# An attention block and a gated MLP on one core: the verdict's bound taken from sums on the squarings, w_out loaded through GpSimd's queue, a new instruction order, and the general path as loops

## The chip, the cores and the metric

The kernel runs on one core of a Trainium2 chip. A core has five engines with queues of their own: TensorE (PE in the profile; its weight loads are PEld), VectorE (DVE), ScalarE (ACT), GpSimd (POOL) and SyncE (SP), which here only issues DMAs. The metric is the device time of one execution, in microseconds; it is the median of three runs.

## What is computed

```python
def _attn_ref(x, inducing):            # x: 4 x 12416 x 128, inducing: 32 x 128
    def mab(q, kv):
        s = scale * (q @ kv.transpose(0, 2, 1))
        s = s - s.max(-1, keepdims=True)
        a = np.exp(s)
        a /= a.sum(-1, keepdims=True) + 1e-09
        return a @ kv
    h = mab(I, x)                      # 32 rows h for each of the 4 batches
    return mab(x, h)                   # each token of x attends to the 32 rows of h

def _moe_ref(x, w_gate, w_val, w_out): # 128 -> 1536 -> 128, on all 49664 tokens
    gate = np.maximum(x @ w_gate, 0.0)
    val = x @ w_val
    return gate * val @ w_out
```

All inputs and the output are float32.

## The kernel before

**The method.** A token's attention output is a convex combination of the 32 rows of h, with weights p. The MLP of it has a product of two linear terms, and a relu. The kernel assumes that each of the 1536 gate units has one sign for all rows of h of a batch; then relu drops out and the output is a quadratic form in p. It is written with squares of differences p_i - p_k, of which there are 16 x 32 for a token, times a table T that depends on the batch alone. So the work is done in two parts. For each batch: the sums over all tokens that give h ("centre"), gates and values of the 32 rows (`gates`, `values`), products of them (`product`, tiles U), `joined` (adds the two halves of U, or leaves the sum to TensorE), `table` (matmuls with wo into T), and a linear part (`lin`, tiles lt, then L). For each block Q of 2048 tokens (24 of them, and one block for the four remainders): the scores s2, `s2_exp` (p on ScalarE), p squared (pp), the normaliser z and its reciprocal (zr), the differences by a matmul with a constant matrix (`differences`, for j = 0 to 3, four PSUM banks each), their squares F, and `outputs` (17 matmuls for each quarter of the block), which `divide` scales into osb, and a store.

**Who squares.** Of the four banks of a (Q, j), the tile dd holds two, which ScalarE squares in one instruction (`sq_two`). Each of the other two (`sq_one`) is squared by ScalarE, or cast by VectorE to SBUF and multiplied there by GpSimd or VectorE (`sq_mul`).

**The verdict.** The assumption on signs is verified while the kernel runs: `extreme` takes the largest absolute score of each block (rng, VectorE); `ext1` to `ext3` make a bound on the scores into a condition on the gates; `other` looks at sums and reciprocals; `count` and `verdict` write one number, left. At the end every engine loads left and branches: if it isn't zero, `general_kernel` computes everything again without the assumption. With these inputs the branch skips it.

**The order.** Within the main stage the order on each engine isn't left to a scheduler. `Plan.add` registers each step with the engines that may run it, the steps that must come before, and the buffer slots that it uses. `ORDER`, a long string of base-64 digits that was made outside the kernel, lists the steps in order, with the engine and the slot of each, and fillers (matmuls that only keep TensorE's clock up, `keep_busy`). Each engine works through its own list in order.

**The start.** `first_batch` handles batch 0: x comes in parts on SP's queue as float32, GpSimd and ScalarE cast it, TensorE turns it and makes the sums. Behind x on SP's queue come w_gate, w_val and w_out as float32 (three tiles w32), which are cast to wg, wv and wo:

```python
        nc.gpsimd.tensor_copy(out=wg, in_=w32[0])
        load_x(1, 0, x16q[0])
        nc.gpsimd.tensor_copy(out=wv[:, 0:half], in_=w32[1][:, 0:half])
        nc.scalar.copy(out=wv[:, half:], in_=w32[1][:, half:])
        for q in range(1, NQ + 1):
            load_x(1, q, x16q[q] if q < NQ else x16r[1])
            if q == 2:
                nc.gpsimd.tensor_copy(out=wo, in_=w32[2].rearrange("p (i c) -> p i c", c=P))
```

`load_x` reads x of the next batch through GpSimd's queue, with a cast to float16 on the way; SP turns it by DMA transposes. The tiles of the main stage (pool mp: ga, va, U, p, F, gm and others) take the memory of `first_batch`'s pool sp (x0, w32, p1a) once it is released.

Lines of the profile that are spoken of: 415, 417, 418, 422 the casts of the weights; 207 `load_x`; 771 `gates`; 785 the gate means gm; 490 `s2_exp`; 503 `extreme`; 541 `differences`; 550 `sq_two`; 555 and 557 `sq_one` on ScalarE and VectorE; 561 `sq_mul`; 569 and 581 `outputs`; 591 `divide`; 361 and 905 ScalarE's exponentials of the first batch and its share of the tables; 874 `product`; 888 `joined`; 893 `table`; 1008 in `other`; 1026 `verdict`; 1278 the branch.

Of the kernel before, what the change touches and what calls it, by code (L numbers as in the profile page):

```python
# [81 lines left out]
0W00X0KV4A1j201t004531K021v11x21V011u10Y01y31W00q4Ka4B0Z21X01Y01n004521Z223O0011L01o11M03P2KH0110f4
3Q2KC0001p11N0KI12V0421O21KD1KJ012X11a021r11b02W21c01d0KR0101e2KE05KS11P041f4KF2KM002KK22Y322300051
KN1KT012522411Q0KW0122631R0KX11S0KO001T2271KY02KP22E051U4KU22F0KZ22u0040A29012v12w2Kn32A0Kb002Ko312
y22B02x3Kc12G02i0040B2H02m1Kd022z32I232k12C02P00Ke22j12D22Z052Ku302K042a22L0K+332J4Kj22M02o00219Kk2
2N02b32p1L432Kl052O202Q0LA342R0Km22s12S02c00347LG352q149010LM32g12d12e2NC02NF042T22f3NE1N805NH14+03
2N922U4NG1NB2N400501NA23E04N52N72ND1330551304-24B1340N623503604A23R00234NJ32+0037223V12-03S1300310N
S239013T14D0303F03G0NR23H03d005253A03I21NL33e13B03C0322NK33D23X004003843f24C323Z1520123J43Y15323b23
g34E23h23jA05463c25p0113l1NT23k13n23i35r14S90038NW24T1LN45q23o34U14W24GA0253NM33p044H14K2Kp42NV2NN0
14I1NU2Kv413q0NQ243003r04M00351NO24X3K-404404N13s04Q23u024L33t233v04O13+05L544NP13-0Ne24Y004324004Z  # L90
1410NI2Kq011LB4342205s313w0Kr13x04504c24a1Nf054F3Ks01542NY2Ng0LH455H0034BNj1Kt24d34603y25L1NZ01Na05
I14723z44R37T050Kw004Nd24845J15B00209NX2Kx14e015D14p035F2Nq37V14f04g04h05C17U2L00144q04i224r0L114s0
5N002074t21L2055P14j015R25O14k0Nk2Nr04Ns0550032A5G2Nv1Ky005S35915725t0414l05614m0Kz24u025u25834n26e
0325w00046L324o46g1Nl017W325+25y1Nm0L60155x16f2LV3LI0045v34v05-2L714w0LW314x0Np160000344y2LJ1L805Lc
336415e01622Li304z46i0406115Y02L926336j25j035f05g0Nw266000555k06k36716A25l0Lo325m05h05n23LC0146B368
15T055i2LD15U06h306C003005o4LE046D16G28I011Lu345V0LF25W08K16H26x000426E15Z05X205a06y15b06-26T036U05
c27036z16V06r005438J25d47X0226N006s16t26O06P07Y26Q06v16u26l001586R227Z36Y026m16p26I046Z06n18L316W07
1000516X216J0731970126q37526K07216L06a06M26b0763LO0139917m000576c2LP1LK046S47n1982LQ036d47C02L+35LL
27D07o17q2M439W0014B7I00LR29X17r39a29B05177039C27809Y1LS27a004599D37909b37b17c27A0LT017B237J07e17K0
7d27L07g0043ALU27E07k17F07N057i17O09A307P07h17M207Q0O603N-047R2O71O301O81Nx00O22O417S4O027s00530Ny2  # L100
O517G27u19y0107w27H48M0207t1Nz27x3O12M549+18N28PA0535N+2OB27y048Q1OJ27z0LX467+07-08R1OI28V002048T18
1058W180228O3OC3820Ld478309z284087038X1OA38528808Z18b00416890Lj498c18f28A08C02OD38B218D08d18E08h005
019-22Lp488F08g38i18l2An011OE038G28j19E004088m2Lv4AAp1LY002OF29F18s05Ao28t08u0OO28v0OG1L-4B9G1Ar012
8y03LZ18z08w20Le0149I18n02O928H4Lf1864OK28o09K0050291049L1OL28p08q09209O1As2Aq319308r2940La0195238x
4A3000238+0At2A71A52Lk0048-0A41Lb2Lg02A639M2Ll1Lq0109029N39Q00150Lh2Lr1Lm049649U29R1Bc032Ls02Ln29V2
Lw0009S1Lt2A900547OM2Lx1A00209n01AD19s00A12OH2Be19o0Ly02AA1Bd2A239p09t09u0Lz2Au0043AOP2M0012Aw19v0O
N29q0Ay1OQ04M11OR09r21Oh3OV0OW03Av1OX09w2OY0OZ0OU29x4AB2AF002199h00Oa2AG1AJ29i09j09k0AH1M6004BA0053
1Ob2M71Oi01BE1Oj09l22BB1Oc02Od0Om2AK2M8049c03Og2BC2AL000159d0On2AN19e09f0AM1CR020Bf20M2059g2BD3AP1M
32Bg0019m4B400354M92CT1Bh2MA2B51AC2MB01CS2Bi3Ah04B81MC2Ai0B61A+00026Aj0B01AR05A-1AS0B22Oo03AT0AU0Op
2B33Or2Ew001Oq2Bj0012BAV20Ey1Oz03Ak0Bn1Bl2BR05O+1BS0Al23Bk1Bm3BT0BU0Ex2Os02Ow01O-1Ov2BG04Ox1Ot2BV21  # L110
Bp00032Oy1BH0P02Br1BI0BJ0Ou2Bq1BL01BK22BM0BN0PD2Bt1BO0B-00508AW02C31P12AX0C01BP2AY0AZ0Ac04PA2BQ4C11
Ad0Bv00300Ae0CU22Bx1DG012Bz2Af0Bw1BW05P82BX0BY0DI1CY00303Ag2Ez31BZ0CZ1DH2Am4B+3Cc2Ca1DTA0415Aa2Cd3C
A00DU1Ba2Ab4CG03PE2DX1Bb4CB0CC0Cq00257DV1DK010P92CD0Cu1CL04Cr1CM0CE22CV052CN0CO0DL2CH0Cs1CW2P22CI0C
k00019PB2CJ0Cl1C505CK23CX3PM0C60DJ30C70Cm1C80CP2Ce00231PG0Co2PH00CQ4Ci1PI0PC2Cf1PJ0PK0E5040P32PL1DN
00134PF2Cg1PN00DO1PO0DR2Cp3PP0PQ0E71DP2Df00236P43PY0PR2DA01Dg1E62DB0PS3C92P500Dj1Dh1CF4EO0045AP62Cw
03EP1Cx0ES2DC0DD0P71Cy0EQ1DE20EC00258Cz0ET3ED1PT00C+21PU0C-04EG1PX2DZ0013BDS2EE1D500DQ2Da1Db2D60E83
2D70D80Ga052Dd1D92EU00212Dc3Gc1D00D10DF4EV1D20Gb2Ge031PZ00Gf2Pa0EY1DM2D32Gn00530EW1Pb0Gp2D44Dq01Go1
Gr2Pc0Dw04Pd2Gt00257Gq2Dx0Gs2Gu1Dy0Gv2Dz0Dl03D+23Gx1Gw3Dm0FJ00029Dn0FK1FN2Do0E9042D-05EA2FO3Dp22E00
FL1F700241E10F81F92E20Gd30Dr0Ds0E32Dt0FB1EI00303FA3Du2E44Fl020EJ1EM2Dv4E+050E-2Fn1EN2FD90416EB2Pe2E
K1FE1FF2F03El90Pi2Eq05FH1Fy0034BEr0FG3Fz1F+2Es0Et0Em0Fm2En0G01Eo0F-3Eu20G200135Ef02G31Ep2Eg0Eh0Gg2E  # L120
i0Ev4G61Ea04Ej21G41F100504Fo32Eb0F21F32Ec0HP031Ed0F42HR1G800218Ee2F51GC2G91Fp052Ek4FU04Fq2GD2FV0FW0
GA1HQ2Fr3Ho00012FX0Hp1Hq2Ff05Fg0FY23Fh0Hs1Fi0HW0023AHr2Fa00Fj22HX1Fb0Fc0Fd0Ha1FP04Fe2HY1Fs00153FQ0H
S21Fk4Ft1Ju030Fw2FR0FS0Fu1Fx2Gh00024FT2Jw1GJ05Gi1Jv2FZ4GK0Gj2GL0GM0Gl1Hi00149Gk3GN20HT030GU00Hj1HU2
GV0Hm2GW0GX0Hk1HV2Gz00256Hn3GY21GP03G+1H12GQ0GR0GS0G-2J3042H23Hc00101GT2J51GE05Hd1H03He2GF0GZ4GG0GH
0J42IE021Hg1Hf3JS00313GI2IG1HJ04JW2JT1GO4HK0J632HL0IF2HM0Hu00JU1HN22JX3JA00518H802Pf2JB1H90JE2HA0HB
0JC1Hv0HC23Hw0JF3JM00345Hx0JN1JO2HE01HF0Hy21HG0JQ1HH0IX0052BJP2I303HI2IZ1I40Ib1I50HO4I60H300IY1I720
H40H50Jx20H60J7042Hz01H72JG00524J82H+0HD4JI1J93H-0I00JH1I803I12I90IA0IH21JK1IB0I24IL00046IC2Jy051Jo
01IM1IN2Jp0ID4Jq0Jd02Jz2IP1IO2Id00300J+3Jj05Ie1If2Je0Jf0Ih2Jg0JY04Jh22IR00307JZ0Ig2IS1Ja0Ii2Jb0II02
0Jr0Jc2Jk0IT1Jl0Jm0IJ2IV1Ji4Js23Pg04IK3J-00322Ph2Ij00K31Io01K01Jn2Ik0Ip0Iq0Pj2Jt4Ir0K12Il0Im0Is21Iu
02Iv0In2Iw0Ix0Iz04K22It4Iy20I+0I-0J00K505J12K60K70K80J24Pk03K922Pl2KA4Pm4"""  # L130


# [5 lines left out]
def square_body(ctx, tc, x, inducing, moe_w_gate, moe_w_val, moe_w_out, out):  # L138
# [100 lines left out]
    def first_batch(sp, psum):  # L239
# [179 lines left out]
        for q in range(1, NQ + 1):  # L419
            load_x(1, q, x16q[q] if q < NQ else x16r[1])  # L420
            if q == 2:
                nc.gpsimd.tensor_copy(out=wo, in_=w32[2].rearrange("p (i c) -> p i c", c=P))  # L422
# [887 lines left out]
```

## Time and profile before

| | |
|---|---|
| median of three runs | 269.79 us (269.72 to 269.85) |
| the profiled execution | 270.34 us, its span 268.6 us |
| granted TensorE clock, mean | 0.945 |
| busy: PE, DVE, ACT, POOL | 239.6, 229.3, 198.7, 124.3 us |
| first divide (line 591) | at 52.47 us |
| last divide ends | at 261.1 us |
| read from and written to HBM | 27.80 and 25.43 MB |

The span is the time between the first and the last instruction of the profiled execution. A row of a group reads: line, engine, operation, output <- inputs, shapes, count, then busy us, mean ns of one, and the idle time of the engine just before with what ended it.

### The profile page before, as it was taken

The numbers are of one execution on the slowest core, as the hardware profiler recorded it, in microseconds if no ns is written. First come the engines' busy times: TensorE is split into PE (matmuls) and PEld (weight loads), VectorE is DVE, ScalarE is ACT, GpSimd is POOL, SyncE is SP. The second block draws the span as 40 slices with busy tenths as digits, with TensorE's granted clock in tenths as the row PEclk, the third lists the DMA queues.
The fourth block names the chain that finished last, engine by engine and source line by source line (L and its number), as shares of the span: only waits on it lengthen the run. The fifth ranks groups of instructions, "written<-read, shape, count | busy, mean of one in ns | idle before, by whom it ended". The sixth has DMA issues, their size and how long they took to land.

```text
span 268.6 us, 9038 instructions
## 1 busy us (share of the span) xinstructions
PE 239.6 (89%) x3825; PEld 170.3 (63%) x3825; DVE 229.3 (85%) x468; ACT 198.7 (74%) x321; POOL 124.3 (46%) x146
## 2 busy tenths in 40 slices
PE   6797588999996889999989999999999989999980
PEld 2685235577662467777756878675767656667770
DVE  4655899976799998978999999999988998997980
ACT  3564677775877358878898798899989889987710
POOL 4456604334875947765655244224483631380000
PEclk9999559999998589999999999999999999999995
DMA  7999994995899589999989992104423224333462
GB/s 254 414 397 272 207 214 93 263 246 153 182 265 243 172 190 194 329 201 276 301 257 214 198 368 93 78 2 195 198 81 124 87 109 159 159 156 159 187 270 68
DMA packets 52624, 53.90 MB, mean 201 GB/s; under 512 B 39744, under 2 KB 41952, under 8 KB 52576
## 3 DMA queue, kind: packets, MB, share of 16 engines
q1 hardware_dynamic: 49504, 43.69, 52.0%
q0 software_dynamic: 3024, 9.54, 19.2%
q8 instruction: 32, 0.52, 0.8%
q14 instruction: 16, 0.13, 0.2%
q10 hardware_dynamic: 48, 0.02, 0.0%
HBM read 27.80 MB, written 25.43 MB: 198 GB/s over the span
## 4 chain that ended last, share of the span: by engine, by line
PE 53%; DVE 28%; DMA 8%; ACT 4%; issue 2%; SPq 1%; POOL 1%; DVEq 0%; ACTq 0%; POOLq 0%
PE mb L581 25%; DVE U L874 8%; PE mb L569 8%; PE dd L541 7%; DMA x<-in_x_dram 6%; DVE osb L591 5%; DVE F L557 4%; PE mb L671 2%; DVE U L888 2%; ACT F L550 2%; PE mb L893 2%; PE mb L686 2%; PE mb L481 2%; DMA xT<-x16q 2%; DVE rng L503 1%
## 5 line engine op out<-in xcount | busy, mean ns | idle before, releaser
L550 ACT ACTIVATE F<-dd 128x1024 f16<-128x1024 f32 x97 | 99.7, 1028 | 22.6 <-PE mb L541 19.8
L581 PE MATMUL mb<-T,F 128*128 128x128 f16 x1552 | 113.8, 221 | 0.0
L581 PEld LDWEIGHTS <-F 128*128 128x128 f16 x1552 | 96.3, 99 | 22.9 <-issue 11.3
L561 POOL TENSOR_TENSOR F<-F 128x512 f16<-128x512 f16 x50 | 56.0, 1127 | 52.8 <-DVE F L557 49.0
L555 ACT ACTIVATE F<-mb 128x512 f16<-128x512 f32 x118 | 68.7, 602 | 11.8 <-PE mb L541 11.6
L591 DVE TENSOR_TENSOR osb<-mb,zr 128x512 f32<-128x512 f32 x97 | 65.1, 682 | 9.8 <-PE mb L581 7.3
L557 DVE CAST F<-mb 128x512 f16<-128x512 f32 x76 | 51.0, 679 | 4.0 <-PE mb L541 3.5
L541 PE MATMUL dd<-p,diff 32*128 32x512 f16 (+1 forms) x200 | 39.0, 389 | 4.7 <-ACT F L550 4.4
L541 PE MATMUL mb<-p,diff 32*128 32x512 f16 (+1 forms) x200 | 41.7, 390 | 1.5 <-DVE F L557 0.9
L569 PE MATMUL mb<-L,pp 128*128 128x512 f16 x96 | 37.3, 389 | 1.1 <-ACT va L826 0.3
L500 POOL TENSOR_TENSOR pp<-p 128x512 f16<-128x512 f16 x16 | 18.7, 1170 | 28.1 <-PE mb L569 27.4
L541 PEld LDWEIGHTS <-diff 32*128 32x128 f16 x400 | 11.6, 91 | 20.1 <-issue 12.3
L529 POOL TENSOR_TENSOR zr<-zr 128x16 f32<-128x16 f32 (+1 forms) x17 | 5.4, 320 | 31.1 <-DVE zr L524 31.0
L490 ACT ACTIVATE p<-mb 128x512 f16<-128x512 f32 (+1 forms) x25 | 15.0, 602 | 5.7 <-POOL wo L422 3.0
L893 PE MATMUL mb<-wo,U 128*128 128x128 f16 x252 | 18.1, 228 | 1.0 <-DVE U L888 0.5
L503 DVE TENSOR_REDUCE rng<-mb 128x1 f32<-128x512 f32 (+1 forms) x25 | 16.6, 666 | 2.0 <-ACT p L490 2.0
L893 PEld LDWEIGHTS <-U 128*128 128x128 f16 x252 | 15.6, 102 | 4.0 <-DVE U L888 2.2
L569 PEld LDWEIGHTS <-pp 128*128 128x128 f16 x97 | 9.6, 99 | 7.9 <-issue 7.7
L676 ACT ACTIVATE p<-mb 128x512 f16<-128x512 f32 (+1 forms) x21 | 11.4, 553 | 3.2 <-PE mb L671 3.1
L342 DVE COPY xT<-xT_ps 128x1024 f16<-128x1024 f16 (+1 forms) x15 | 8.5, 582 | 5.7 <-PE xT_ps L341 5.6
L351 POOL CAST x16f<-x 128x512 f16<-128x512 f32 (+2 forms) x15 | 8.5, 564 | 9.8 <-DMA x<-in_x_dram 9.8
L561 DVE TENSOR_TENSOR F<-F 128x512 f16<-128x512 f16 x26 | 11.4, 447 | 0.1
(143 smaller groups left out, 308.5 us busy)
## 6 DMA issues: line engine op xcount, KB each, us to landing
out_dram<-osb SPq DMA_DIRECT2D x48, 512.0 KB, 3.2
x16q<-in_x_dram POOLq DMA_DIRECT2D x18, 512.0 KB, 10.5
x<-in_x_dram SPq DMA_DIRECT2D x9, 512.0 KB, 6.8
x<-in_x_dram SPq DMA_DIRECT2D x6, 256.0 KB, 9.3
w<-in_moe_w_gate_dram SPq DMA_DIRECT2D x1, 768.0 KB, 8.4
w<-in_moe_w_val_dram SPq DMA_DIRECT2D x1, 768.0 KB, 9.2
w<-in_moe_w_out_dram SPq DMA_DIRECT2D x1, 768.0 KB, 9.6
xT<-x16q SPq DMA_TRANSPOSE x18, 4.5
```

The lines of the kernel that those rows point to most:

```text
L500: engines[e].tensor_tensor(out=p2b[slot["pp", Q]][:, 0:w], in0=a, in1=a, op=ALU.mult)
L503: dve.tensor_reduce(out=rng[:, Q : Q + 1], in_=mb[slot["m", "s2", Q]][:, 0 : width(Q)], axis=AX.X, op=ALU.max, apply_absolute_value=True,)
L541: nc.tensor.matmul(bs[r][:, o], diff[rows, 4 * jj : 4 * jj + 4, :].rearrange("p k m -> p (k m)"), pb[slot["p", Q]][rows, 0:w], start=True, ...
L550: act.activation(out=Fb[slot["F", Q, j]][:, 0:2, :], in_=dd, func=AF.Square)
L555: act.activation(out=dst, in_=src, func=AF.Square)
L557: dve.tensor_copy(out=dst, in_=src)
L561: engines[e].tensor_tensor(out=a, in0=a, in1=a, op=ALU.mult)
L569: nc.tensor.matmul(ps, p2b[slot["pp", Q]][:, tok], tab.rearrange("p r c -> p (r c)"), start=True, stop=False,)
L581: nc.tensor.matmul(ps[:, r * P : (r + 1) * P], lhsT, T[r if rest else Q // NQ][:, j, :], start=False, stop=(r, j) == (3, 3),)
L591: dve.tensor_tensor(out=o[:, 4 * (t % 2) : 4 * (t % 2) + 4, :], in0=mb[slot["m", "o", Q, t]].rearrange("p (r c) -> p r c", r=4), in1=zr[sl ...
L874: engines[e].tensor_tensor(out=U[i][:, :, k0 - 1 : k0 + 6 : 2, :], in0=a[:, :, 0:M].unsqueeze(2).broadcast_to([P, NFF, 4, M]), in1=win, op ...
L893: nc.tensor.matmul(ps, U[i][:, t, 4 * j : 4 * j + 4, :].rearrange("p k m -> p (k m)"), wo[:, t, :], start=(i, t) == (0, 0), stop=(i, t) == ...
```

## The change

- **The verdict's bound.** `extreme` goes. Instead, ScalarE's squarings of dd for j = 2 and j = 3 also give the sum of what they write (`accum_out`), one column of rng each: 48 instructions, and three for the remainder block, 51 in all. `ext1` adds all the columns and makes the bound from that. For the sums to cover all four rows r, dd holds rows 2 and 3 where j is odd. `ext1` now needs the squarings of j = 2 and 3 of all blocks, the remainder's too. `other` comes after `ext1`, and also takes the largest reciprocal; for that zr is one tile for all blocks instead of three in turn.
- **The weights.** w_out isn't loaded on SP any more; GpSimd's queue loads it with a cast, straight into wo. wv is cast by ScalarE alone. The loads of batch 1 all follow wo's.
- **The order.** ORDER is another string. Counted over the main stage: VectorE casts 66 banks instead of 76 and joins 6 tables instead of 8; GpSimd multiplies 40 F instead of 50 and squares 14 p instead of 16; VectorE squares 10 p instead of 8; ScalarE squares 128 single banks instead of 118; TensorE has 264 table matmuls instead of 252 and 20 fillers instead of 22. For batch 0 all four joins are TensorE's. Seven fillers stand right before the verdict's last matmul. `other` stands in VectorE's list after `ext1`, which comes with four divides left, and before the last three divides; the rest of the verdict comes behind them.
- **The general path.** `general_kernel` has loops on the chip over tiles of 128 tokens, where it was unrolled. On TensorE the program now has 7,772 instruction rows, it had 26,697; about 7,640 of them come before the branch in both.

```diff
-    rng = const([P, B * NQ + 1], FP32, "rng")
+    rng = const([P, 2 * B * NQ + 3], FP32, "rng")
...
-        nc.sync.dma_start(
-            out=w32[2].rearrange("p (i c) -> p i c", c=P),
-            in_=moe_w_out.rearrange("(i p) c -> p i c", p=P),
-        )
...
         nc.gpsimd.tensor_copy(out=wg, in_=w32[0])
-        load_x(1, 0, x16q[0])
-        nc.gpsimd.tensor_copy(out=wv[:, 0:half], in_=w32[1][:, 0:half])
-        nc.scalar.copy(out=wv[:, half:], in_=w32[1][:, half:])
-        for q in range(1, NQ + 1):
+        nc.gpsimd.dma_start(out=wo, in_=moe_w_out.rearrange("(i p) c -> p i c", p=P))
+        nc.scalar.copy(out=wv, in_=w32[1])
+        for q in range(NQ + 1):
             load_x(1, q, x16q[q] if q < NQ else x16r[1])
-            if q == 2:
-                nc.gpsimd.tensor_copy(out=wo, in_=w32[2].rearrange("p (i c) -> p i c", c=P))
...
-    def extreme(Q, e):
-        dve.tensor_reduce(
-            out=rng[:, Q : Q + 1],
-            in_=mb[slot["m", "s2", Q]][:, 0 : width(Q)],
-            axis=AX.X,
-            op=ALU.max,
-            apply_absolute_value=True,
-        )
...
     def d_banks(Q, j):
-        return [dd[:, 0, :], dd[:, 1, :], *(mb[slot["m", "d", Q, j, r]] for r in (2, 3))]
+        two = [dd[:, 0, :], dd[:, 1, :]]
+        ones = [mb[slot["m", "d", Q, j, i]] for i in range(2)]
+        return two + ones if j % 2 == 0 else ones + two
...
     def sq_two(Q, j, e):
-        act.activation(out=Fb[slot["F", Q, j]][:, 0:2, :], in_=dd, func=AF.Square)
+        k = {2: 0, 3: 1}.get(j) if Q < B * NQ else 0
+        act.activation(
+            out=Fb[slot["F", Q, j]][:, pair(j), :],
+            in_=dd,
+            func=AF.Square,
+            accum_out=None if k is None else spread(Q, k),
+        )
...
     def sq_one(Q, j, i, e):
         if e == "ACT":
-            act.activation(out=dst, in_=src, func=AF.Square)
+            more = {"accum_out": spread(Q, 1 + i)} if Q == B * NQ else {}
+            act.activation(out=dst, in_=src, func=AF.Square, **more)
         else:
             dve.tensor_copy(out=dst, in_=src)
...
     def ext1(e):
-        r = pos[:, 0:1]
-        dve.tensor_reduce(out=r, in_=rng, axis=AX.X, op=ALU.max)
-        small(dve, r, r, sm_scale / HS * (1 + 2.0**-7), ALU.mult, 100.0, ALU.min)
+        r, q = pos[:, 0:1], tsum[:, B + 1 : B + 2]
+        dve.tensor_reduce(out=q, in_=rng, axis=AX.X, op=ALU.add)
+        small(dve, r, q, 2.0**12 * 2.5, ALU.mult, 2.0**-12 * 2.5, ALU.add)
+        small(dve, r, r, 100.0, ALU.min)
         small(dve, ext, eye32, r, ALU.mult)
...
     def other(e):
+        c = chk[:, NCHK - 1 : NCHK]
+        dve.tensor_reduce(out=c, in_=zr[:, :, 0, :], axis=AX.XY, op=ALU.max)
+        small(dve, c, c, 1.0 / (HS * 0.9 * M), ALU.is_le)
         z = rzs.rearrange("p b m -> p (b m)")
...
-    add(("ext1",), "DVE", [("rng", Q) for Q in range(B * NQ + 1)], [], ext1)
+    seen2 = [("f2", Q, j) for Q in range(B * NQ) for j in (2, 3)]
+    seen2 += [("f2", B * NQ, 0)] + [("fc", B * NQ, 0, i) for i in range(2)]
+    add(("ext1",), "DVE", seen2, [], ext1)
...
-    add(("other",), "DVE", seen + [("centre", b) for b in range(B)], [], other)
+    seen += [("zr", Q) for Q in range(B * NQ + 1)] + [("centre", b) for b in range(B)]
+    add(("other",), "DVE", seen + [("ext1",)], [], other)
...
 def general_kernel(tc, x, inducing, moe_w_gate, moe_w_val, moe_w_out, out):
...
-        for b in range(B):
-            for t0 in range(0, NT, CT):
...
+        with tc.For_i(0, B * N, N, **LOOP) as first:
+            with tc.For_i(0, N, P, **LOOP) as t:
+                _, xT = tile_of(first + t)
```

More of the change, by code (lines that the diff above doesn't have):

```diff
@@ L82 @@
[L82 to L86, printed above, removed]
@@ L453, in square_body @@
     Fb = [mt([P, 4, BLK], FP16, f"F{i}") for i in range(NF)]
-    zr = [mt([P, 2, 16], FP32, f"zr{i}") for i in range(3)]
+    zr = mt([P, B * NQ + 1, 2, 16], FP32, "zr")
     p1b = [mt([P, CT, M], FP16, f"p1_{i}") for i in range(2)]
@@ L646, in square_body @@
                 add(("o", Q, t, r), "PE", deps, [om] + ([] if r else [pp]) + Fs, f(outputs, t, r))
[L647 removed]
+            add(("e", Q, t), "DVE", [("o", Q, t, 3), ("zq", Q)], [om, ok], f(divide, t))
             if t % 2 or rest:
@@ new lines, in general_kernel @@
+        with tc.For_i(0, B * N, N, **LOOP) as first:
+            nc.vector.memset(top, -3e38)
+            nc.vector.memset(acc, 0.0)
+            with tc.For_i(0, N, P, **LOOP) as t:
+                _, xT = tile_of(first + t)
+                ps = bank("a", [M, P])
+                nc.tensor.matmul(ps, indT, xT, start=True, stop=True)
+                new = st([M, 1], FP32, "gnew")
+                nc.vector.tensor_reduce(out=new, in_=ps, axis=AX.X, op=ALU.max)
+                nc.vector.tensor_tensor(out=top, in0=top, in1=new, op=ALU.max)
```

418 lines of the change are left out of this document (186 added, 232 removed).

## The prediction

> **What bounds the kernel now.** I read the page first (busy shares and the chain that ended last), then the busy time by stretch, then the waits, then the order of time at the two ends.
>
> ```profile
> span 268.6 us, 9038 instructions
> PE 239.6 (89%) x3825; PEld 170.3 (63%) x3825; DVE 229.3 (85%) x468; ACT 198.7 (74%) x321; POOL 124.3 (46%) x146
> PE 53%; DVE 28%; DMA 8%; ACT 4%; issue 2%; SPq 1%; POOL 1%; DVEq 0%; ACTq 0%; POOLq 0%
> ```
>
> The last row is the chain that ended last, by engine: TensorE (PE) and VectorE (DVE) hand it to one another, ScalarE (ACT) hardly has a part. Where each leads is seen in the stretches:
>
> ```profile
> core 0: us, PE busy (x) PEld busy (x) DVE busy (x) ACT busy (x) POOL busy (x), PEclk, DMA share, GB/s
> 0.00:28.00 28.00, 21.46 (x376) 15.79 (x376) 14.52 (x41) 13.37 (x33) 15.62 (x31) 0.99 0.95 330
> 28.00:50.00 22.00, 17.22 (x178) 8.74 (x179) 21.83 (x40) 16.76 (x29) 6.75 (x11) 0.71 0.90 181
> 50.00:120.00 70.00, 64.55 (x1147) 46.50 (x1145) 60.51 (x112) 49.80 (x79) 44.78 (x48) 0.93 0.96 219
> 120.00:240.00 120.00, 115.84 (x1820) 82.69 (x1820) 114.33 (x237) 106.29 (x165) 55.35 (x54) 1.00 0.57 173
> 240.00:261.20 21.20, 20.52 (x314) 16.57 (x311) 18.09 (x42) 12.49 (x18) 1.81 (x4) 1.00 0.45 183
> 261.20:268.60 7.40, 0.00 (x0) 0.00 (x0) 0.00 (x0) 0.00 (x0) 0.00 (x0) 0.61 0.30 98
> ```
>
> From 28 to 50 us VectorE is full (21.83 of 22.00) while TensorE runs at a granted clock of 0.71. From 50 to 240 us VectorE and TensorE are both nearly full, ScalarE is third. From 240 us on TensorE alone leads. In the last 7.4 us nothing computes. So VectorE work taken away is worth all of itself at the start, a part of it in the middle, nothing near the end. What it can be worth at most is what TensorE has left: idle time plus the time lost to the clock, 4.8 + 22 x 0.29 = 11.2 us in 28 to 50, 5.5 + 70 x 0.07 = 10.4 us in 50 to 120, 4.2 us in 120 to 240.
>
> **Part 1: wo leaves SP's queue and GpSimd's cast.**
>
> ```profile
> DVE gm L785 <- POOL wo L422: 2.7, 1, 2.7
> ACT p L490 <- POOL wo L422: 3.0, 1, 3.0
> 22.23 1.47 POOL L415 CAST wg<-w 128x1536 f16<-128x1536 f32 x1 [1.48 <-DMA w<-in_moe_w_gate_dram]
> 23.64 0.72 POOL L207 DMA_DIRECT2D x16q<-in_x_dram  x1
> 26.64 1.47 POOL L422 CAST wo<-w 128x1536 f16<-128x1536 f32 x1 [0.45 <-DMA w<-in_moe_w_out_dram]
> 24.28 0.83 ACT L418 CAST wv<-w 128x768 f16<-128x768 f32 x1 [1.40 <-DMA w<-in_moe_w_val_dram]
> 25.61 0.60 PE L771 MATMUL mb<-hT,wg 128*128 128x81 f16 x12 [1.55 <-DVE hT L237]
> 28.14 0.17 DVE L785 COPY gm<-mb 128x6 f32<-128x6 f32 x1 [2.67 <-POOL wo L422]
> 52.47 0.68 DVE L591 TENSOR_TENSOR osb<-mb,zr 128x512 f32<-128x512 f32 x1
> x16q<-in_x_dram POOLq DMA_DIRECT2D x18, 512.0 KB, 10.5
> ```
>
> The main stage's buffers lie where the weights' float32 copies lay, so VectorE and ScalarE begin only when the last cast has read them: gm's product is there at 25.61 + 0.60 = 26.2 us, but gm starts at 28.14. With no wo cast, the last reader is ScalarE's cast of all of wv. Half of it took 0.83 us; twice that, 1.66, is the upper bound: 24.28 + 1.66 = 25.9 us, still before 26.2. So gm starts at about 26.3: 1.8 us saved. What covers the longer cast is the centring on VectorE and the first gates on TensorE; without that cover it costs 0.8 us.
>
> GpSimd's queue after the wg cast: wo's issue, then seven loads of x. Nothing stands between them any more, so at 0.55 to 0.72 us an issue GpSimd is free near 28.5 us. wo's 768 KB now pass ahead of batch 1's x in that queue; a 512 KB (1 MB read) load lands 10.5 us after its issue in the median. wo is cut in 12 pieces a partition. For its issue I have rows of one piece a partition only: lower bound 0.72, upper bound 12 x 0.55 = 6.6 us; I take 1, since the DMA's size makes no difference to the issue in the rows that I have. wo's first reader is the first table matmul. Its products need three more VectorE multiplications after the gates, so it can't start before about 32 us; with 23.6 + 1 + about 5 wo is there before. I cost this at nothing; the cover is 2 to 3 us deep. On SP the queue loses one issue; batch 1's transposes there wait for its last load and come about as late as before.
>
> **Part 2: the reductions of the scores go, sums ride on the squarings, ten casts change engine.**
>
> ```profile
> L503 DVE TENSOR_REDUCE rng<-mb 128x1 f32<-128x512 f32 x24 | 16.3, 682 | 2.0 <-ACT p L490 2.0
> L557 DVE CAST F<-mb 128x512 f16<-128x512 f32 x76 | 51.0, 679 | 4.0 <-PE mb L541 3.5
> L555 ACT ACTIVATE F<-mb 128x512 f16<-128x512 f32 x118 | 68.7, 602 | 11.8 <-PE mb L541 11.6
> L888 DVE TENSOR_TENSOR U<-U,U 128x1536 f16<-128x1536 f16 x8 | 7.7, 970 | 0.0
> L905 ACT ACTIVATE T<-mb,half 128x128 f16<-128x128 f32 x6 | 2.2, 372 | 2.1 <-PE mb L893 2.0
> L490 ACT ACTIVATE p<-mb 128x128 f16<-128x128 f32 x1 | 0.3, 285 | 0.0
> L361 ACT ACTIVATE p1a<-s_ps 128x32 f16<-128x32 f32 x1 | 0.2, 200 | 0.0
> L1008 DVE SCALAR_TENSOR_TENSOR chk<-rzs,chk 128x128 f32<-128x128 f32 x1 | 1.1, 1097 | 0.0
> ```
>
> VectorE loses 24 x 0.68 + 0.3 = 16.6 us of reductions, 10 casts (76 become 66) x 0.67 = 6.7, two joins of tables (8 become 6) x 0.97 = 1.9, and gains some 3 us (two products of p, two of the linear part, the new check). From 28 to 261.2 us it was busy 214.8 us; that becomes 193, a tenth less. ScalarE gains 10 squarings x 0.58 = 5.8 us and 51 sums. No sum on a squaring is in this trace. Its price: not below nothing, since the squaring reads and writes what it did; the nearest pair of rows is one more operand of one column, 372 - 285 = 0.09 us; the upper bound is an instruction of its own, 0.20 us by the smallest ScalarE row, and 0.1 for the overlap lost behind it. I take 0.09, so 51 x 0.09 = 4.6 us (0 to 15). ScalarE's 185.4 us of 28 to 261.2 become 196: level with VectorE. TensorE's work stays (12 table matmuls more, two fillers less).
>
> By stretch. **28 to 50:** up to the first divide VectorE has 29 instructions in the new order against 41: no reduction of scores, no join (TensorE sums both halves itself), two checks of the tables later. At the mean durations that is 19 us against 27; the 27 took 52.47 - 28.14 = 24.3, so the 19 take 17, and the divide could come at 26.3 + 17 = 43 us. ScalarE's squarings and the half clock do not follow that fast: it has 18 us of work from about 26.8 us until the eighth squaring. I take 47 us: 5.5 us saved, the 1.8 of part 1 in it (bounds 3 and 9). **50 to 120:** VectorE was at 86% with full spells; some 8 us leave, 2 us come that were put off; TensorE has 10.4 us to give. I take 2.5 (0 to 6). **120 to 240:** TensorE has 4.2 us to give, and ScalarE goes from 106 to some 111 of 120. I take 2 (0 to 4). **240 to 261:** nothing.
>
> **Part 3: the end.** Here the change speaks against itself.
>
> ```profile
> 254.29 0.23 PE L541 MATMUL dd<-p,diff 32*128 32x128 f16 x2
> 255.26 1.02 ACT L550 ACTIVATE F<-dd 128x1024 f16<-128x1024 f32 x1
> 260.99 0.15 DVE L1026 TENSOR_SCALAR left<-mb 128x1 int32<-128x1 f32 x1
> L1278 POOLq COMPARE_BRANCH  x1: 45/45/45, 262.1 to 262.1; - x1
> L1278 PEldq COMPARE_BRANCH  x1: 3431/3431/3431, 262.1 to 262.1; - x1
> L1278 DVEq COMPARE_BRANCH  x1: 72/72/72, 262.1 to 262.1; - x1
> L1278 POOLq EVENT_SEMAPHORE  x1: 17/17/17, 262.6 to 262.6; - x1
> L1278 PEldq EVENT_SEMAPHORE  x1: 51/51/51, 265.6 to 265.6; - x1
> L1278 SPq EVENT_SEMAPHORE  x8: 17/17/17, 266.3 to 266.9; - x8
> ```
>
> The verdict's bound was ready early; now it needs the last block's squarings. Call the start of that block's differences D (254.29 before; the verdict left was done at D + 6.9). New order: three sums on ScalarE until D + 3.0; four small VectorE instructions, 0.8; a divide, 0.7; the other checks, which wait for the bound, 1.10 for the row of line 1008 and about 1.9 for six more, 3.0; three divides behind them, 2.0; the rest of the verdict, 1.7, and 0.5 for TensorE and the comparison: D + 11.7. That is 4.8 us later, 4.4 with the overlap that VectorE's rows show. Behind the checks in VectorE's queue stand the last divides; their store waits, but it lands while the verdict is still under way.
>
> After the verdict each engine branches over the general path. TensorE's branch took 3.43 us, GpSimd's and VectorE's 0.05 and 0.07, and SP's closing waits came 0.7 us after TensorE passed. In the programs the branch skips some 19,000 TensorE instructions before and some 130 after; GpSimd skipped a few dozen. I take it that the length is the cause, and that 3.4 us go. Net at the end: +1.0 (bounds -0.5 and +5). The Trainium skill, "Runtime: NRT & Kernel Launch", Instruction fetch mechanics, says that a taken branch to a target outside the two pages loaded has to fetch it first; TensorE's 3431 ns against GpSimd's 45 agree, and by that rule the stall goes with the length too.
>
> **Sum.** -5.5 - 2.5 - 2 + 1.0 = -9.0. The profiled execution took 270.34 us for its span of 268.6; the median is 269.79. 270.34 - 9.0 = 261.3, and 0.55 less for the median: **260.8 us**.
>
> **Rivals.** *ScalarE becomes the bound.* For: it gets both the casts and the sums. It would be as full as VectorE was if a sum cost (214.8 - 185.4 - 5.8) / 51 = 0.46 us, beyond my upper bound of 0.3. There only the start is kept, about 268; at 0.3 about 265. Chance 0.12 for 0.3 and over.
>
> *The branch's 3.4 us stay*, being something else than the skipped length: 260.8 + 3.4 = 264.2. Chance 0.10.
>
> *wo comes late, and it is slower.* TensorE works in order, so a table matmul that waits for wo holds the differences behind it, at half clock. It decides once wo lands after about 32 us, one us for each us, and the loads of x move back with it. If the issue takes 6.6 us, wo lands near 36 and batch 1's x 5 to 6 us later: 4 + 5. If writing or moving the pieces takes 12 us more, the start is lost and batch 1 waits: +11 to 260.8, 272. Against: wo went through SP's queue in the same pieces and was there by 26.6. The Trainium skill, "SBUF — State Buffer", Who interferes with whom, says that VectorE in a two-port mode keeps GpSimd from writing descriptors until it is done; by that rule wo is held only behind the short VectorE instructions of 23 to 26 us, and no row shows such a hold. Chance 0.08.
>
> *The new order starves TensorE at a batch's start.* The clock of 0.93 in 50 to 120 shows what a hole costs: 4.9 us for two stretches. Two more such holes with their idle time, and the middle loses what it won and 8 more: 273. Chance 0.08.
>
> **Numbers.** Forecast 0.62 (255 to 266, from the bounds of the terms), the others as given. A measurement of this kernel can tell about 0.2% (0.5 us) from no change. Faster: 0.62 + 0.10 + 0.07 of the first rival = 0.79; within 0.2%: 0.02; slower: 0.16 + 0.03 = 0.19. The range of 255 to 270.5 leaves out the last two rivals and a few hundredths below.
>
> **What would show it.** gm right after its product, near 26.3; no wait on wo; the first divide by 47; a squaring with its sum within 0.1 us of one without; VectorE near 207 us in all and ScalarE near 209; TensorE's branch under 0.1 us; left about 11 us after the last block's differences. It is wrong if TensorE waits on wo's DMA, if ScalarE is full from 120 to 240, or if the clock falls anew.

## The result and the profile after

The changed kernel took 266.78 us in the median (265.62 to 267.24, 4 runs) against 269.82 of the kernel before (269.72 to 269.86): a ratio of 0.988, 95% interval 0.985 to 0.991. So it is faster by 1.2%, where 3.3% were forecast. The direction was right, the time lies 0.8 us beyond the 255 to 266 us of the forecast itself and within the wide range, and the steps did not add up to it. Ratios, here and below, leave out executions more than 1.5% above the fastest of their kernel and compare with executions of the kernel before taken beside them (medians of 269.8 to 270.2 us).

The page of the changed kernel, its span, the engines and the chain that ended last, by engine:

```profile
span 264.8 us, 9054 instructions
PE 236.7 (89%) x3835; PEld 170.4 (64%) x3835; DVE 211.8 (80%) x439; ACT 207.1 (78%) x382; POOL 105.2 (40%) x132
PE 42%; DMA 30%; DVE 17%; SPq 5%; issue 2%; POOL 2%; ACT 1%; DVEq 0%
```

Compare the last row with its counterpart before (PE 53, DVE 28, DMA 8). VectorE and ScalarE came out near the forecast, 211.8 and 207.1 us of work (207 and 209 were named). But the chain's share of transfers went from 8% to 30%: TensorE and VectorE each gave up 11 points, and DMA took them. The table of stretches, with the columns of the one before, says where:

```profile
28.00:50.00 22.00, 20.03 (x282) 12.99 (x281) 17.85 (x30) 18.80 (x34) 8.22 (x11) 1.00 0.86 169
50.00:120.00 70.00, 61.04 (x1105) 44.63 (x1104) 51.38 (x104) 53.35 (x98) 22.98 (x29) 0.95 1.04 222
120.00:240.00 120.00, 113.87 (x1793) 81.50 (x1791) 107.52 (x212) 107.25 (x193) 53.49 (x54) 0.99 0.63 177
```

In 28 to 50 us TensorE does 20.0 us of work at the full clock, where it did 17.2 at 0.71. In 50 to 120 us TensorE does 61.0 us of work (64.6 before), VectorE 51.4 (60.5) and GpSimd 23.0 (44.8); only ScalarE has more, 53.4 (49.8). When an engine gets lighter and TensorE does less in the same stretch, something else is waited for. What waited for DMA, from the view of the waits (engine, line, what it waited for; us in all, times, the longest):

```profile
POOL seen L660 <- DMA xT<-x16q: 10.8, 1, 10.8
DVE osb L590 <- DMA out_dram<-osb: 10.2, 3, 4.5
PEld L673 <- DMA xT<-x16q: 8.8, 6, 3.9
PE mb L673 <- DMA xT<-x16q: 7.6, 4, 3.8
```

Line 660 is GpSimd's step ahead of the loads of the third batch, which waits for the second batch's transposes. Line 673 holds the first score matmuls of a new batch: TensorE waits for the transposed x. In the kernel before the two rows of this line read 1.4 and 1.2 us, and the other two rows are not there. The queue that carries the transposes, in the changed kernel (start, duration on SP's queue, count; a row of several holds the waits between them too):

```profile
44.21 2.06 SPq L664 DMA_TRANSPOSE xTr<-x16r  x1
46.38 16.35 SPq L664 DMA_TRANSPOSE xT<-x16q  x6
...
91.35 2.51 SPq L664 DMA_TRANSPOSE xTr<-x16r  x1
93.92 0.57 SPq L605 DMA_DIRECT2D out_dram<-osb  x1
94.59 8.98 SPq L664 DMA_TRANSPOSE xT<-x16q  x3
103.66 0.53 SPq L605 DMA_DIRECT2D out_dram<-osb  x1
104.30 6.27 SPq L664 DMA_TRANSPOSE xT<-x16q  x2
110.66 0.94 SPq L605 DMA_DIRECT2D out_dram<-osb  x1
111.70 4.35 SPq L664 DMA_TRANSPOSE xT<-x16q  x1
```

and in the kernel before, at the same turn from the second batch to the third:

```profile
93.04 1.13 SPq L662 DMA_TRANSPOSE xTr<-x16r  x1
94.27 13.88 SPq L662 DMA_TRANSPOSE xT<-x16q  x6
```

The compute of the changed kernel was 7.1 us ahead at its first divide (45.38 us for 52.47), but the transposes are not: for the third batch they start at 91.35 instead of 93.04, and for the fourth at 146.85, later than the 138.39 of before. Their first is the small one of the last 128 rows (`xTr`), whose load is the last of seven on GpSimd's queue, so the six large ones wait until everything has landed. Meanwhile the DMA engines drain (share 0.10):

```profile
90.00:95.00 5.00, 4.00 (x38) 2.77 (x39) 2.74 (x4) 2.58 (x7) 1.85 (x2) 0.73 0.10 24
```

Then stores stand between the transposes, and a store that stands behind a transpose holds back its buffer, for which the divides wait.

The chain that ended last has these transfers in it, in order of time (start, us):

```profile
27.32 16.87 DMA x16r<-in_x_dram
94.59 5.19 DMA xT<-x16q
103.66 4.61 DMA out_dram<-osb
110.66 5.62 DMA out_dram<-osb
131.53 15.31 DMA x16r<-in_x_dram
```

Here the waits for the small load itself stand ahead of the second and the fourth batch. At the turn to the third batch the chain has a transpose and two stores that stood behind transposes. The large transposes there also wait for TensorE, 18.5 us in all between 85 and 120 us.

### The profile page after: what moved, and what is told of

Its sections match the earlier page's. It is cut to its first block, busy times and chain, and to the rows that moved or that the text cites. A ratio compares the mean times of both kernels' runs of the same rounds, so it can differ in the third digit from the quotient of the medians.

```text
span 264.8 us, 9054 instructions
## 1 busy us (share of the span) xinstructions
PE 236.7 (89%) x3835; PEld 170.4 (64%) x3835; DVE 211.8 (80%) x439; ACT 207.1 (78%) x382; POOL 105.2 (40%) x132
## 4 chain that ended last, share of the span: by engine, by line
PE 42%; DMA 30%; DVE 17%; SPq 5%; issue 2%; POOL 2%; ACT 1%; DVEq 0%
PE mb L580 20%; DMA x16r<-in_x_dram 12%; DMA xT<-x16q 6%; PE mb L568 5%; SPq L664 5%; DMA x<-in_x_dram 5%; DVE osb L590 5%; DVE U L876 4%; PE dd L528 4%; DMA out_dram<-osb 4%; PE mb L528 4%; DMA w<-in_moe_w_val_dram 3%; PE mb L895 2%; PE mb L673 2%; PE mb L688 2%
## 5 line engine op out<-in xcount | busy, mean ns | idle before, releaser
L580 PE MATMUL mb<-T,F 128*128 128x128 f16 x1552 | 116.0, 222 | 0.0
L580 PEld LDWEIGHTS <-F 128*128 128x128 f16 x1552 | 97.3, 99 | 21.1 <-issue 9.4
L590 DVE TENSOR_TENSOR osb<-mb,zr 128x512 f32<-128x512 f32 x97 | 64.6, 682 | 14.2 <-DMA out_dram<-osb 10.2
L554 ACT ACTIVATE F<-mb 128x512 f16<-128x512 f32 x128 | 73.3, 605 | 3.3 <-PE mb L528 1.9
L560 POOL TENSOR_TENSOR F<-F 128x512 f16<-128x512 f16 x40 | 41.8, 1050 | 66.2 <-DVE F L556 55.5
L556 DVE CAST F<-mb 128x512 f16<-128x512 f32 x66 | 44.5, 683 | 11.9 <-PE mb L528 9.0
L491 POOL TENSOR_TENSOR pp<-p 128x512 f16<-128x512 f16 x14 | 16.9, 1209 | 18.8 <-ACT p L481 11.6
L890 POOL TENSOR_TENSOR U<-U,U 128x1536 f16<-128x1536 f16 x4 | 12.4, 3107 | 28.6 <-DVE U L876 28.6
L678 ACT ACTIVATE p<-mb 128x512 f16<-128x512 f32 (+1 forms) x21 | 11.2, 550 | 10.8 <-PE mb L673 9.5
L673 PE MATMUL mb<-indT,xT 128*128 128x32 f16 x288 | 10.1, 177 | 8.0 <-DMA xT<-x16q 7.6
L673 PEld LDWEIGHTS <-xT 128*128 128x128 f16 x288 | 8.8, 96 | 9.1 <-DMA xT<-x16q 8.8
L560 DVE TENSOR_TENSOR F<-F 128x512 f16<-128x512 f16 x26 | 14.0, 545 | 0.1
```

Of the source, the lines that this page charges most:

```text
L491: engines[e].tensor_tensor(out=p2b[slot["pp", Q]][:, 0:w], in0=a, in1=a, op=ALU.mult)
L554: act.activation(out=dst, in_=src, func=AF.Square, **more)
L556: dve.tensor_copy(out=dst, in_=src)
L560: engines[e].tensor_tensor(out=a, in0=a, in1=a, op=ALU.mult)
L580: nc.tensor.matmul(ps[:, r * P : (r + 1) * P], lhsT, T[r if rest else Q // NQ][:, j, :], start=False, stop=(r, j) == (3, 3),)
L590: dve.tensor_tensor(out=o[:, 4 * (t % 2) : 4 * (t % 2) + 4, :], in0=mb[slot["m", "o", Q, t]].rearrange("p (r c) -> p r c", r=4), in1=zr[:, ...
```

## The experiments

**VectorE's relief alone, in the old order (before_no_max).**

```diff
     def extreme(Q, e):
-        dve.tensor_reduce(
-            out=rng[:, Q : Q + 1],
-            in_=mb[slot["m", "s2", Q]][:, 0 : width(Q)],
-            axis=AX.X,
-            op=ALU.max,
-            apply_absolute_value=True,
-        )
+        if Q == 0:
+            dve.memset(rng, 0.0)
```

> The kernel before, in its own order, with the 25 maxima of the squared scores left out (the row of the bound is set to zero once): VectorE loses 25 instructions, 16.6 us. It leaves out the measurement on which the verdict rests. Theory A (my forecast's premise: VectorE's load sets the pace of the middle): the relief is two thirds of the change's 25 us, so two thirds of the terms that I put on VectorE, about -5 to -6 us: 264 to 265 us. Theory B (between 48 and about 160 us the middle runs at the pace of the transfers, which keep the DMA engines at a share of 1.0, and only the start and the last 90 us run at VectorE's pace): the start gains 1 to 2 us and gives it back, the last 90 us gain 1 to 3: 267 to 269 us.

Measured: 268.53 us, ratio 0.992 (0.989 to 0.995): -1.7 us for 16.6 us of VectorE's rows. Its busy time fell by 11.4 us only, from 229.3 to 217.9: rows of one engine overlap, and VectorE's add up to 256 us in the kernel before. Theory A, the premise of my forecast, falls for the old order, and the time is in theory B's range. 6.3 us more than before is now idle time ahead of its divides, most of it for TensorE:

```profile
L586 DVE TENSOR_TENSOR osb<-mb,zr 128x512 f32<-128x512 f32 x97 | 65.1, 683 | 16.1 <-PE mb L576 11.8 <-POOL pp L500 1.1 <-POOL F L556 1.0
```

(Before, it was 9.8 us idle ahead of the divides, 7.3 of it for TensorE.)

**The transposes of two turns left out, in both kernels (after_no_turn, before_no_turn).**

```diff
     def turn(b, q, e):
+        if b > 1 and q < NQ:
+            return
```

> The changed kernel without the twelve large transposing transfers of the third and fourth batch: those batches compute on the transposed blocks that stand in the buffers from the two batches before. Order, engines and all other steps as in the changed kernel. Theory B (the transfers at the turn of a batch are what the middle waits for): TensorE's idle time of 6.3 us in 90 to 120 and 4.3 us in 140 to 160 goes, and what is behind it at a lower clock: -7 to -11 us, 256 to 260 us. Theory C (the new order itself starves the engines there, whatever the transfers do): the waits change their names and little is gained, 264 to 266 us.

> The same omission in the kernel before: no large transposing transfers for the third and fourth batch. Theory B: its TensorE waits for transposes only 1.2 us in all and VectorE is busy in the same stretch, so little is gained, -1 to -3 us: 267 to 269 us; the difference between this gain and that of the changed kernel is what the change paid at the turns. Theory A: none of it matters here either, 269 to 270 us.

Measured: the changed kernel 254.74 us, ratio 0.942 (0.937 to 0.947); the kernel before 269.94 us, ratio 0.999 (0.997 to 1.002). The same omission is worth 12 us in the one and nothing that can be measured in the other. With the transposes out of the way the change is worth 269.9 - 254.7 = 15.2 us; with them it is worth 3. TensorE at the two turns, in the changed kernel without these transposes:

```profile
90.00:120.00 30.00, 27.32 (x511) 19.95 (x512) 23.84 (x46) 25.09 (x45) 15.05 (x19) 1.00 0.54 160
140.00:165.00 25.00, 25.00 (x491) 18.42 (x488) 22.39 (x47) 22.96 (x42) 9.37 (x8) 1.00 0.32 126
```

and with them:

```profile
90.00:120.00 30.00, 23.68 (x411) 17.10 (x412) 17.78 (x34) 17.90 (x32) 9.41 (x12) 0.89 0.94 199
140.00:165.00 25.00, 20.68 (x398) 15.06 (x398) 17.15 (x32) 18.80 (x35) 9.93 (x8) 0.93 0.99 188
```

3.6 and 4.3 us of TensorE's work are missing in the two stretches, and the clock is at 0.89 and 0.93 instead of 1.00. Theory B holds for the changed kernel, theory C falls. For the kernel before theory B is not right as I had put it: the DMA engines are just as full there in the same two stretches (0.93 and 1.01), and yet next to nothing waits for the transposes:

```profile
90.00:120.00 30.00, 28.31 (x533) 21.37 (x534) 26.91 (x44) 20.10 (x33) 21.20 (x22) 0.91 0.93 208
140.00:165.00 25.00, 24.72 (x510) 18.72 (x508) 24.91 (x46) 21.01 (x34) 11.94 (x10) 1.00 1.01 231
```

**The small loads of two batches early (after_x16r_early).** No work is left out here: the 32 KB loads of the third and fourth batch are only issued earlier, right behind that of the second.

```diff
         for q in range(NQ + 1):
             load_x(1, q, x16q[q] if q < NQ else x16r[1])
+        for b in range(2, B):
+            load_x(b, NQ, x16r[b])
...
     def load(b, q, e):
+        if q == NQ:
+            return
```

> The changed kernel with the small loads (the last 128 rows) of the third and fourth batch issued at the start, behind the second batch's loads; the step in which they were issued does nothing. In the changed kernel each batch's first transpose is that of the small block, whose load is the last of seven on GpSimd's queue, so all six large transposes wait until everything has landed (91.35 and 146.85 us, with the DMA engines at a share of 0.09 to 0.13 in 90 to 94 and 0.03 in 146 to 148). Theory B: the transposes can start when the first large load has landed, some 10 us earlier, TensorE's waits of the turns shrink by half or more: -3 to -6 us, 261 to 264 us. Theory C: no change within 0.5 us, 266.3 to 267.3 us; 1.1 us more on GpSimd near 28 us cost nothing, since it idles until 37 us there.

Measured: 257.91 us, ratio 0.953 (0.948 to 0.959): 9 us less than the changed kernel, more than expected. SP's queue at the same turn:

```profile
80.21 1.13 SPq L668 DMA_TRANSPOSE xTr<-x16r  x1
...
82.08 16.38 SPq L668 DMA_TRANSPOSE xT<-x16q  x3
```

The transposes begin at 80.2 instead of 91.4 us, while the loads are still landing, and the waits fall:

```profile
PEld L677 <- DMA xT<-x16q: 3.3, 3, 1.8
DVE osb L592 <- DMA out_dram<-osb: 3.0, 3, 2.5
PE mb L677 <- DMA xT<-x16q: 2.9, 3, 1.7
```

from 8.8, 10.2 and 7.6 us. The last of the six large transposes ends at 110.9 instead of 116.1 us at this turn and at 156.9 instead of 165.6 at the next. So most of the loss, 9 of the 12 us, hung on the one small load that the first transpose of a batch waits for. SP's waits for TensorE stayed (22.1 us between 60 and 120 us), so they are not what the 9 us were.

**Is it the order that makes the relief worth something? (before_no_max_no_turn)**

> The kernel before without the 25 maxima and without the twelve large transposing transfers of the third and fourth batch (those batches compute on older blocks). Each omission alone gave -1.7 and -0.2 us. Theory D (transfers became the bound as soon as VectorE was relieved, in the old order too): together -5 us or more, 262 to 265 us. Theory E (in the old order TensorE and VectorE wait for each other step by step, so 16.6 us off VectorE are worth little there with or without transfers; the change's gain comes from the new order that is planned for the lighter VectorE): together -1.5 to -2.5 us, 267.5 to 268.7 us.

Measured: 267.97 us, ratio 0.992 (0.990 to 0.995). Theory D falls: even without the large transposes at the turns the old order makes 2 us of the 16.6 of rows. Theory E's number stands. Its reason, that the order written for a heavier VectorE hands work to and fro with TensorE so that neither gets ahead, is my reading of the waits; no run isolates it. With the 1.0 and 1.6 us of the next two runs, the parts tried alone in the old order make under 5 of the 15.2 us. The rest comes with the new order, the casts and joins that it moves, and what the parts are worth together; which of these gives how much was not tried.

**Part 1 alone (before_wo_pool).**

```diff
-        nc.sync.dma_start(
-            out=w32[2].rearrange("p (i c) -> p i c", c=P),
-            in_=moe_w_out.rearrange("(i p) c -> p i c", p=P),
-        )
...
-        load_x(1, 0, x16q[0])
-        nc.gpsimd.tensor_copy(out=wv[:, 0:half], in_=w32[1][:, 0:half])
-        nc.scalar.copy(out=wv[:, half:], in_=w32[1][:, half:])
-        for q in range(1, NQ + 1):
+        nc.gpsimd.dma_start(out=wo, in_=moe_w_out.rearrange("(i p) c -> p i c", p=P))
+        nc.scalar.copy(out=wv, in_=w32[1])
+        for q in range(NQ + 1):
...
```

> The kernel before with the change's part 1 alone: the output weights by GpSimd's own queue straight to half precision, their transfer on SP's queue and GpSimd's cast gone, the value weights cast by ScalarE alone, the second batch's loads behind the output weights. My forecast's part 1: the gate means start 1.8 us earlier, of which this order keeps what VectorE's chain allows: -1 to -2 us, 268 to 269 us. Theory B adds that the second batch's loads and transposes move by under 2 us and that nothing waits for them in the old order: no loss from them. If part 1 makes the transposes late enough to cost at the first turn: 270 to 272 us.

Measured: 268.98 us, ratio 0.996 (0.993 to 0.998), -1.0 us. The gate means start at 25.56 instead of 28.14 us, the first divide at 50.83 instead of 52.47; the second batch's first transpose moves back, from 42.81 to 44.77 us, and costs nothing that shows here:

```profile
25.56 0.16 DVE L777 COPY gm<-mb 128x6 f32<-128x6 f32 x1 [0.74 <-ACT wv L412]
50.83 0.68 DVE L583 TENSOR_TENSOR osb<-mb,zr 128x512 f32<-128x512 f32 x1
...
44.77 1.19 SPq L654 DMA_TRANSPOSE xTr<-x16r  x1
```

**Part 3's loops alone (before_loops).** The function of the general path is the changed one; the verdict is the old one.

> The kernel before with the general path of the changed kernel (loops on the chip): nothing else is changed. The branch on TensorE, 3.43 us at the end before, should take 0.5 us: -3.0 us if it sets the end, 267.0 to 267.5 us. If the end is set by the closing events of the other queues, which the long branch only delayed in part: -1 us, 269 us.

Measured: 268.42 us, ratio 0.995 (0.992 to 0.998), -1.6 us, and 2.0 between the two profiled spans. The last store's issue, TensorE's branch, VectorE's first event behind its own branch, and SP's closing events (the last three by source line: duration min/median/max in ns, first and last start):

```profile
261.05 0.38 SPq L602 DMA_DIRECT2D out_dram<-osb  x1
...
L1234 PEldq COMPARE_BRANCH  x1: 236/236/236, 262.1 to 262.1; - x1
L1234 DVEq EVENT_SEMAPHORE  x1: 21/21/21, 265.5 to 265.5; - x1
...
L1261 SPq EVENT_SEMAPHORE  x14: 17/28/683, 264.3 to 266.6; - x14
```

3.2 us of branch went, 2.0 came off the span. Two things ended next. SP's closing events begin at 264.3, when the last store has landed (issued at 261.05 + 0.38 us, about 2.8 us to landing: 264.2). The one of 683 ns runs from 264.9 to 265.6, and VectorE's event comes only at 265.5, 3.4 us after its branch (262.1). So it is most likely VectorE that SP waits for last; the profile doesn't name it. In the kernel before, VectorE's first event came 4.2 us and ScalarE's 4.0 us after their branches; here ScalarE's comes after 0.4 us, and in the changed kernel they come after 0.6 and 0.2 us. Why VectorE is still late here, with the short path, is open.

**The sums on the squarings left out (after_no_sums).**

```diff
             func=AF.Square,
-            accum_out=None if k is None else spread(Q, k),
...
-            more = {"accum_out": spread(Q, 1 + i)} if Q == B * NQ else {}
+            more = {}
...
+    pool.memset(rng, 0.0)
```

> The changed kernel with its order and without the 51 sums on ScalarE (the row of the bound is zero): it leaves out the measurement on which the verdict rests. ScalarE loses 10.2 us of read rows, of which each delays the next squaring by 0.1 us. With the turns' transfers setting the pace (theory B) nothing comes of it before 165 us: 266.0 to 267.2 us, no change. If the sums were what was lost in the middle (theory S), 3 to 5 us come back: 261.5 to 263.5 us.

Measured: 266.11 us (265.71 to 268.5), ratio 0.988 (0.983 to 0.994): no difference from the changed kernel that can be measured. Theory S falls.

**A fifth output buffer (after_osb5).**

```diff
-    NP, NF, NO, NM = 3, 12, 4, 6
+    NP, NF, NO, NM = 3, 12, 5, 6
...
+                if k[0] == "osb":
+                    free = [j for j in range(self.rings["osb"]) if ("osb", j) not in used]
+                    i = min(free, key=lambda j: self.freed.get(j, -1))
```

> The changed kernel with five output buffers instead of four, handed out in turn (the one that has been free longest); nothing else. In the changed kernel VectorE's divides waited 10.2 us in three places for a buffer whose store stood behind transposes on SP's queue. If those stores are the loss (theory B2), most of it goes: -4 to -6 us, 261 to 263 us. If the transposes' own lateness is the loss (theory B1), TensorE waits for them instead: -0.5 to -2 us, 265 to 266.3 us.

Measured: 265.0 us, ratio 0.981 (0.976 to 0.986), 1.8 us under the changed kernel's median, with overlapping intervals. The divides' row is gone from the waits, and TensorE's has grown:

```profile
PE mb L679 <- DMA xT<-x16q: 10.1, 6, 2.9
```

10.1 us instead of 7.6: most of the wait only moved, as theory B1 says.

**All small loads first, in both kernels, and with the fifth buffer (after_all_early, before_all_early, after_all_early_osb5).**

```diff
+        load_x(1, NQ, x16r[1])
+        for q in range(NQ):
+            load_x(1, q, x16q[q])
+        for b in range(2, B):
+            load_x(b, NQ, x16r[b])
...
     def load(b, q, e):
+        if q == NQ:
+            return
```

> As the run with the small loads at the start (257.9 us), and the second batch's own small load ahead of its large ones: its first transpose need not wait for all seven loads (44.2 us) either. Theory B1: the transposes of the second batch start some 8 us earlier, GpSimd's wait of 10.7 us for their end shrinks and with it the third batch's loads move ahead: another -2 to -4 us, 254 to 256 us, about what the kernel without transposes at the two turns took (254.7). If the loads themselves, not their start, set the pace by then (DMA share 1.1 in 50 to 90): 257.5 to 258 us, nothing more.

> The same edit in the kernel before (small loads first, for all batches). There leaving the transposes out altogether was worth -0.2 us, so theory B expects nothing: 269.4 to 270.2 us, although SP's transposes start some 8 to 12 us earlier. If earlier transfers are worth something in any order: -3 us or more, 267 us.

> Both edits in the changed kernel: all small loads first and five output buffers. The divides' waits for a buffer were 3.0 us in all with the small loads of two batches early. Theory B1: those 3 us are in part on the chain (a store's 4.67 us from issue to landing stood in it at 106 to 111 us): -1 to -2 us against the same kernel with four buffers, 253 to 255 us. If nothing is left there: the same within 0.5 us.

Measured: the changed kernel with the small loads first 256.88 us (253.52 to 257.85), ratio 0.945 (0.937 to 0.953); with five buffers as well 255.57 us (253.41 to 256.63), ratio 0.944 (0.936 to 0.951), the fastest of all. Against the run with two batches' small loads early (0.953) the intervals overlap, so what these two additions bring is not settled. For the second batch the premise of theory B1 failed. In the run with five buffers its small transpose starts at 28.88 instead of 44.21 us and the large ones at 32.07 instead of 46.38, but they spread out:

```profile
32.07 27.46 SPq L675 DMA_TRANSPOSE xT<-x16q  x6
```

The last ends at 59.5 instead of 62.7 us, and GpSimd still waits 9.6 us for it (10.8 in the changed kernel). At this turn the small load held up the start far more than the end.

The same edit in the kernel before: 270.43 us, ratio 1.002 (0.999 to 1.004): nothing, though all its small loads come early there too. There the third batch's transposes start at 85.00 instead of 93.04 us, the fourth's at 138.41 instead of 138.39, so only one of the two later turns moved. An edit worth 3 to 4% in the changed kernel is worth nothing in the kernel before.

## Why the prediction was right and wrong

By the profiled executions, with D again the start of the last block's differences:

| stretch | forecast | changed kernel | without the turns' transposes |
|---|---|---|---|
| start to the first divide (52.47 us before) | -5.5 | 45.38: -7.1 | 45.80: -6.7 |
| first divide to D (254.29 us before) | -2.5 - 2 = -4.5 | D 250.54: +3.3 | D 237.81: -9.8 |
| D to the end (14.3 us before) | +1.0 | 14.3: 0.0 | 14.3: 0.0 |
| sum | -9.0 | -3.8 | -16.5 |

```profile
250.54 0.23 PE L528 MATMUL dd<-p,diff 32*128 32x128 f16 x2
```

**The start** was right in its mechanism and 1.6 us too small. gm began at 25.67 us (26.3 forecast), and the first divide at 45.38 (by 47):

```profile
25.67 0.16 DVE L787 COPY gm<-mb 128x6 f32<-128x6 f32 x1 [0.72 <-issue]
45.38 0.69 DVE L590 TENSOR_TENSOR osb<-mb,zr 128x512 f32<-128x512 f32 x1 [0.21 <-PE mb L580]
```

I had held ScalarE and the half clock against the 43 us that VectorE's count gave. The clock was what I misjudged: 1.00 in 28 to 50 us, not 0.71. Where I wrote that the half clock does "not follow that fast", there was no half clock: the granted clock is 1.00 in every stretch from 20 to 36 us, where it had been 0.50 from 28 to 40. TensorE was busy for 1.0, 1.8 and 1.6 us of the three stretches of 2 us from 24 to 30 us, before it was 0.5, 1.2 and 0.6; that this is the reason was not tried.

**The middle is the step that failed**, in its two terms: 2.5 us for 50 to 120 us and 2 for 120 to 240. Instead of winning 4.5 us it lost 3.3. I weighed VectorE, ScalarE and TensorE there, each by its busy time, and put the wait for transfers at nothing, although the row that I quoted for 50 to 120 us has a DMA share of 0.96. On part 1 I even wrote that the second batch's transposes "come about as late as before". That was right, and it was the point: everything else came earlier, so they became late. Without them the middle wins 9.8 us, more than twice my terms; the runs show that the change pays 12 us at the two turns, and that 9 come back when one load per batch no longer gates them; where the other 3 come from is not settled.

The profile before held two warnings. The waits of SP's own queue:

```profile
SPq L662 <- DMA x16r<-in_x_dram: 34.5, 2, 25.2
```

SP's queue stood still for 34.5 us for the small loads, 25.2 of them ahead of the second batch. And the chain that ended last had a transfer in it, at the turn to the third batch:

```profile
94.27 4.46 DMA xT<-x16q
98.77 0.56 PE mb L671 x16
```

TensorE waited 1.2 us for it. A wait that short looked like no cost; but a transfer that is waited for at all has no slack left, and compute that arrives there earlier waits for the difference, as it did in the changed kernel.

**The rival that came nearest** is the one that I gave 0.08: the new order starves TensorE at a batch's start. Its place was right, but its cause was not the order by itself, and its price of 273 us was too high, because the compute had more to give than I had counted. **ScalarE as the bound** did not come: leaving the sums out changed nothing. A sum is a row of its own, 0.20 us, but the next squaring starts 0.09 us after it starts, the value that I took:

```profile
249.91 0.20 ACT L542 ACTIVATION_READ_ACCUMULATOR F<-dd 128x1 f32 x1
250.00 1.08 ACT L554 ACTIVATE F<-mb 128x512 f16<-128x512 f32 x2
```

**wo coming late** did not come either: no wait on it is in the trace.

**The end** came out at 0.0 for +1.0, because the verdict came less late than I had it and the rest was about right. The verdict:

```profile
260.79 0.16 DVE L1034 TENSOR_SCALAR left<-mb 128x1 int32<-128x1 f32 x1 [0.47 <-PE mb L1029]
L1246 PEldq COMPARE_BRANCH  x1: 458/458/458, 261.6 to 261.6; - x1
```

left was done at D + 10.4 (D + 11.7 forecast; the row that I had priced at 1.10 us took 0.29): 3.5 us later than before, where I had 4.4. From left to the end it took 3.9 us instead of 7.5, so 3.6 came off, where I had 3.4. TensorE's branch is not all of that: it took 0.46 us, not under 0.1, and when it went alone only 2.0 us came off the span. I had read the branch rows alone; VectorE's and ScalarE's first events behind theirs were as late as TensorE's in the kernel before (266.3 and 266.0 us against 265.6). That the long path is the cause of TensorE's stall is borne out: with the loops and nothing else changed, 3431 ns became 236. The Trainium skill, "Runtime: NRT & Kernel Launch", Instruction fetch mechanics, says that a taken branch beyond the pages loaded has to fetch its target. TensorE's rows agree with that; VectorE's 3.4 us over the short path in the run with the loops alone are not explained by the length.

## What to carry to other kernels

Before an engine's relief is turned into time, ask of every transfer in that stretch by how much it is early; a wait of about a microsecond on a DMA in the trace before says that its slack is zero. A row of busy times can't show this; the queue's own waits and the transfers in the chain that ended last can. And price an edit in the kernel in which it will run: the same earlier loads were worth nothing in the kernel before and 3 to 4% in the changed one, and leaving out rows of 16.6 us on VectorE brought 1.7 us in the old order.

## What the runs showed of the hardware

A 32 KB load issued behind six of 512 KB on GpSimd's queue took 15.3 us in the median from issue to landing, and the transposes that waited for it left the DMA engines at a share of 0.10 for 5 us. The order of loads within one queue thus set the start of a stage by its smallest member at the two later turns. The eighth and ninth load of x in a row were not issued at once either: in the run with the small loads early GpSimd stood still for 1.02 and 2.66 us ahead of them.

```profile
28.79 0.54 POOL L206 DMA_DIRECT2D x16r<-in_x_dram  x1 [1.02 <-DMA wo<-in_moe_w_out_dram]
31.99 0.53 POOL L206 DMA_DIRECT2D x16r<-in_x_dram  x1 [2.66 <-DMA x16q<-in_x_dram]
```

GpSimd's issue of a load in 12 pieces a partition (wo) took 1.22 us against 0.53 to 0.6 us for the loads of x; I had taken 1, with 6.6 as a bound.

TensorE's branch took 3431 to 3751 ns in the kernels with the unrolled path and 236 to 458 ns in those with loops, while the other engines' took 45 to 72 ns in both. A short branch row doesn't mean that the engine goes on at once: in the kernel before VectorE's and ScalarE's first events behind the branch came 4.2 and 4.0 us after it, GpSimd's 0.5 us. What they waited for is not shown.
